# Beacon attention and soft mixture of experts on one Trainium2 core: V stored as two keys a partition, masks added by TensorE, experts in column groups

## The chip, the cores and the metric

One core of a Trainium2 chip runs the whole program. The metric is device time in microseconds. The engines are TensorE (PE, with its weight loads PEld), VectorE (DVE), ScalarE (ACT), GpSimd (POOL) and SyncE (SP, which issues most DMAs).

## The reference

Attention over 8 batches and 8 heads of 576 tokens with 64 dimensions; 16 beacon keys and values stand ahead of the others and are never masked. Its output, as 4608 rows of 512, is x for a soft mixture of 8 experts with 4 slots each:

```python
k_all = np.concatenate([beacon_k, k], axis=2)          # 592 keys
v_all = np.concatenate([beacon_v, v], axis=2)
scores = scale * np.matmul(q, k_all.transpose(0, 1, 3, 2))
scores = np.where(causal, -1000000000.0, scores)       # causal[:, Nb:] = triu(k=1)
a = softmax(scores, -1)
attn_out = np.matmul(a, v_all)
x = attn_out.transpose(0, 2, 1, 3).reshape(B * S, H * D)
logits = x @ phi                                       # 4608 x 32
d = softmax(logits, 0)                                 # over the tokens
slot_input = (d.T @ x).reshape(E, S_per_e, D)
slot_out[e] = np.maximum(slot_input[e] @ w1[e], 0.0) @ w2[e]    # 512 -> 1024 -> 512
c = softmax(logits, 1)                                 # over the slots
return c @ slot_out
```

## The kernel before

The kernel is one loop over 32 pairs of heads (`n`, four pairs `g` to a batch `b`) and a tail. The instructions of each engine run in the order in which the Python text issues them, so this order is written by hand; engines wait for each other only through the tiles they share.

**Loads.** `load_pair` (L84, DMAs at L88) brings q and k of one pair as 128 partitions of nine rows each, 288 KB a tensor; five pairs are held, and pair n+5 is asked for at the end of pair n. `load_v` (L96, L103) brings V as 128 keys a partition block, 8 heads of 64 values each, so that a DMA moves rows of 256 bytes; a quarter of the next batch is asked for at each pair of the present one. `cast_v` (L241) turns V to 16 bits into `vh`, partly on GpSimd and partly on VectorE, one pair after it was asked for. `load_w` (L109, L120) brings the experts' weights in 32 pieces of 512 KB (as stored in 16 bits), issued by GpSimd; six tiles for w1 and six for w2 hold 24 pieces, and the last eight take the place of pieces that experts 0 and 1 have used.

**A pair.** `transp(n+1)` (L187) transposes the next pair's q and k with 36 products of 64x64 into two PSUM tiles, which VectorE copies (L189) into `qT` and `kT`; GpSimd puts the beacon keys in front (L192). `score` (L202) has four steps, and every step fills one of two PSUM tiles `sc` and is followed by one exp on ScalarE (L208) of 1024, 992, 928 and 416 columns (two heads together). Keys lie on the partitions and queries on the columns. Step 0 holds the four full diagonal blocks, and GpSimd clears their masked half after the exp (L210); step 1 begins with the last diagonal block of 80, cleared at L216. `attend` (L229) multiplies the blocks of `ex` with V for one head of the pair before, 15 products into a PSUM tile `av`; column 64 of V holds ones, so that column 64 of the result is the softmax's sum, and VectorE divides (L236, L237) into `xb`. The order on TensorE in a pair is: score step 0, some routing, score step 1, the next pair's transposes, `attend` of the first head of the pair before, score step 2, `attend` of the second head, score step 3.

**Routing of a batch** runs in the next batch's pairs as seven pieces: three transposing `xb` into `xT` (L256, L261, L265), two for the logits and their exp `eLh` (L271, L275), one transposing that (L283), and `si_piece` (L294, L298), which adds `d.T @ x` to `siacc`.

**Tail.** The column sums for `c` (L373); then for each expert 32 products of w1's blocks with four slots each (L392), Relu into a zero-padded tile `hTz` (L395), and eight products of `hTz` with 512 columns of w2 (L397), all accumulated in one PSUM tile `sop`, which is `avs[0]`. VectorE scales it into `soh` (L401). The output is 36 products of 512 columns (L413), read out by ScalarE and VectorE in turn (L415, L417) and stored by SP in nine groups of four.

Of the kernel before, what the change touches and what calls it, by code (L numbers as in the profile page):

```python
# [17 lines left out]
def kernel(  # L18
# [24 lines left out]
    NP = B * H // 2  # L43
    NDC = Dm // P
    NFC = F // P
    DD = D + 1
    scale = 1.0 / D ** 0.5
    assert Dm == H * D and N == B * S and UL == 80 and J == 9
# [3 lines left out]
    steps = [  # L52
        [(c, P, P * c, P, P * c) for c in range(4)],
        [(4, UL, 4 * P, UL, 0), (3, P, 4 * P, UL, UL), (1, P, 2 * P, U - 2 * P, 2 * UL)],
        [(0, P, P, U - P, 0)],
        [(2, P, 3 * P, U - 3 * P, 0)],
    ]
    width = [512, 496, 464, 208]
    soff = [0, 512, 1008, 1472]
    EW = 1680  # L60
    blk = {}
    for st, pieces in enumerate(steps):
        for (c, kn, u0, un, col) in pieces:
            for i in range(NCH):
                lo = P * i
                if u0 <= lo < u0 + un:
                    blk[(c, i)] = soff[st] + col + lo - u0
    assert len(blk) == 15

    const = ctx.enter_context(tc.tile_pool(name="const", bufs=1))  # L70
    qkp = ctx.enter_context(tc.tile_pool(name="qkp", bufs=5))
    vfp = ctx.enter_context(tc.tile_pool(name="vfp", bufs=6))
    exq = ctx.enter_context(tc.tile_pool(name="exq", bufs=2))
    sml = ctx.enter_context(tc.tile_pool(name="sml", bufs=4))
    wh = ctx.enter_context(tc.tile_pool(name="wh", bufs=6))
# [5 lines left out]

    qf, kf = {}, {}

    def load_pair(n):  # L84
        b, g = divmod(n, H // 2)
        for (d, src, nm) in ((qf, q, "qf"), (kf, k, "kf")):
            t = qkp.tile([P, J, D], FP, name=nm, tag=nm)
            nc.sync.dma_start(  # L88
                out=t[:, :, :],
                in_=src[b, 2 * g:2 * g + 2].rearrange("h s d -> (h s) d").rearrange(  # L90
                    "(p j) d -> p j d", j=J))
            d[n] = t

    vf = {}

    def load_v(b, part):  # L96
        for c in ((0, 1), (2,), (3,), (4,))[part]:
            vf[(b, c)] = vfp.tile([P, H, D], FP, name="vf", tag="vf")
            if c == 0:
                nc.sync.dma_start(out=vf[(b, c)][0:Nb], in_=beacon_v[b].rearrange("h n d -> n h d"))  # L100
            lo, hi = max(0, c * P - Nb), min(S, (c + 1) * P - Nb)
            p0 = lo + Nb - c * P
            nc.sync.dma_start(out=vf[(b, c)][p0:p0 + hi - lo],  # L103
                              in_=v[b, :, lo:hi, :].rearrange("h p d -> p h d"))

    NPC = 4 * E
    w1h, w2h = {}, {}

    def load_w(m):  # L109
        e, r = divmod(m, 4)  # L110
        d, nm = (w1h, "w1h") if r < 2 else (w2h, "w2h")
        if r % 2 == 0:
            d[e] = wh.tile([P, 4096], F16, name=nm, tag=nm)
        o = (r % 2) * 2048
        if r < 2:
            src = moe_w1[e, r * 256:(r + 1) * 256].rearrange("(c p) f -> p c f", p=P)
        else:
            src = moe_w2[e, (r - 2) * 512:(r - 1) * 512].rearrange("(c p) f -> p c f", p=P)
        c = src.shape[1]
        nc.gpsimd.dma_start(  # L120
            out=d[e][:, o:o + 2048].rearrange("p (c f) -> p c f", c=c), in_=src)

    load_pair(0)
    bkf = const.tile([P, B, D], FP, name="bkf")
    nc.sync.dma_start(out=bkf[:, :, :], in_=beacon_k.rearrange("b h n d -> (h n) b d"))
    load_pair(1)
    for part in range(4):
        load_v(0, part)
    phif = const.tile([P, NDC, NSL], FP, name="phif")
    nc.sync.dma_start(out=phif[:, :, :], in_=moe_phi.rearrange("(c p) e -> p c e", p=P))  # L130
    load_pair(2)
    load_pair(3)
    load_pair(4)
# [5 lines left out]
    nc.vector.tensor_copy(out=idh[:, :], in_=idb[:, :])  # L139
    ones = const.tile([P, 1], F16, name="ones")  # L140
    nc.vector.memset(ones[:, :], 1.0)
    qT = [const.tile([P, 5 * P], BF, name=f"qT{i}") for i in range(3)]
    kT = [const.tile([P, 5 * P], BF, name=f"kT{i}") for i in range(3)]
    for i in range(3):
        nc.vector.memset(qT[i][:, 0:Nb], 0.0)
    vh = [const.tile([P, NCH, H, DD], F16, name=f"vh{i}") for i in range(2)]
    for i in range(2):
        nc.gpsimd.memset(vh[i][:, :, :, D:DD], 1.0)
    xb = [const.tile([P, NCH, H, D], F16, name=f"xb{i}") for i in range(2)]
    eLh = const.tile([NSL, Nb + N], F16, name="eLh")  # L150
    nc.vector.memset(eLh[:, 0:Nb], 0.0)
    dsum9 = const.tile([NSL, 2 * B], FP, name="dsum9")
# [4 lines left out]
    phih = const.tile([P, NDC, NSL], F16, name="phih")  # L157
    bkT = const.tile([P, NP, Nb], BF, name="bkT")
# [4 lines left out]
    nc.vector.memset(scs[1][64:P, :, 0:UL], 0.0)  # L163

    def beacons():
# [7 lines left out]
        for r in range(2):  # L173
            nc.vector.tensor_copy(
                out=bkT[64 * r:64 * r + 64, :, :],
                in_=tp[64 * r:64 * r + 64, :, :].rearrange(
                    "p b (g r n) -> p (b g) r n", g=H // 2, r=2)[:, :, r, :])


    def transp(n):  # L180
        for (f, dst) in ((qf, qT[n % 3]), (kf, kT[n % 3])):
            t = f.pop(n)
            tp = ps_tr.tile([P, J, 64], BF, name="tr", tag="tr")
            for j in range(J):
                for po in (0, 64):
                    hi = t[po:po + 64, j, :].bitcast(BF)[:, 1::2]
                    nc.tensor.transpose(tp[po:po + 64, j, :], hi,  # L187
                                        idb[po:po + 64, po:po + 64])
            nc.vector.tensor_copy(  # L189
                out=dst[:, Nb:Nb + S].rearrange("p (s j) -> p s j", j=J),  # L190
                in_=tp[:, :, :].rearrange("p j s -> p s j"))
        nc.gpsimd.tensor_copy(out=kT[n % 3][:, 0:Nb], in_=bkT[:, n, :])  # L192
# [3 lines left out]
    def score(n, st):  # L196
        if st == 0:
            ex[n] = exq.tile([P, 2, EW], F16, name="ex", tag="ex")
        sc = scs[st % 2]
        for (c, kn, u0, un, col) in steps[st]:  # L200
            for a in range(2):
                nc.tensor.matmul(  # L202
                    sc[0:kn, a, col:col + un],
                    kT[n % 3][64 * a:64 * a + 64, P * c:P * c + kn],
                    qT[n % 3][64 * a:64 * a + 64, u0:u0 + un],
                    start=True, stop=True)
        w, o = width[st], soff[st]
        nc.scalar.activation(ex[n][:, :, o:o + w], sc[:, :, 0:w], AF.Exp, scale=scale)  # L208
        if st == 0:
            nc.gpsimd.affine_select(  # L210
                out=ex[n][:, :, 0:512].rearrange("p a (c t) -> p a c t", c=4),
                in_=ex[n][:, :, 0:512].rearrange("p a (c t) -> p a c t", c=4),
                compare_op=AL.is_ge, fill=0.0, base=0,
                pattern=[[0, 2], [0, 4], [1, P]], channel_multiplier=-1)
        if st == 1:
            nc.gpsimd.affine_select(  # L216
                out=ex[n][0:UL, :, o:o + UL], in_=ex[n][0:UL, :, o:o + UL],
# [3 lines left out]
    def attend(n, a):  # L221
        b, g = divmod(n, H // 2)
        h = 2 * g + a
        for i in range(NCH):
            m = P if i < 4 else UL
            for c in range(i + 1):
                kn = P if c < 4 else UL
                o = blk[(c, i)]
                nc.tensor.matmul(  # L229
                    avs[a][0:m, i * DD:(i + 1) * DD],  # L230
                    ex[n][0:kn, a, o:o + m],
                    vh[b % 2][0:kn, c, h, :],
                    start=(c == 0), stop=(c == i))
# [77 lines left out]
    wl = 0  # L311
# [141 lines left out]
```

## Time and profile before

| | |
|---|---|
| runs | 236.87, 238.39 and 239.73 us, median 238.39 |
| profiled execution, span | 239.4 us |
| busy time in it | PE 187.1, PEld 129.1, DVE 130.8, ACT 127.4, POOL 89.4 us |
| DMA | 55.63 MB written, 63,715 packets, 41,920 of them under 512 B |
| first exp, last exp of the loop | start 11.56 us, end 173.4 us |
| experts | from 181.45 to 211.2 us |
| output | from 211.2 us to the end |

The page gives the profiled execution by its span, from the first instruction to the last. Its parts are one execution's; the runs are others. Busy times of engines lie beside each other and don't add up to the span, and a product's length holds a latency that the next one overlaps, so what a run of products costs is read from start to start.

### The profile page before, as it was taken

To read this page: it belongs to the slowest core of one execution; us is meant where nothing else is said; L and a number is where in the kernel's file an instruction comes from. 1 tells how busy PE (TensorE), PEld (TensorE's weight loads), DVE (VectorE), ACT (ScalarE), POOL (GpSimd) and SP (SyncE) were. 2 spreads that over 40 slices of the span, in tenths; PEclk is the share of its full clock that TensorE was granted. 3 is DMA by queue.
4 is the path that set the end of the run, shared out by engine and by line. 5 is a ranking of instruction groups with operands and counts; after the bars stand their busy time and mean duration, and the time that the engine had idled before them with its cause. 6 is when DMAs were issued, how large, how long until landed. Compare 5 with 4: busy or idle time off the path is not lost.

```text
span 239.4 us, 8048 instructions
## 1 busy us (share of the span) xinstructions
PE 187.1 (78%) x3512; PEld 129.1 (54%) x3512; DVE 130.8 (55%) x304; ACT 127.4 (53%) x187; POOL 89.4 (37%) x161
## 2 busy tenths in 40 slices
PE   0579778869986898797898698899869999979800
PEld 0457566647664766575666476677646445532200
DVE  4583967555777566777667666566652000058800
ACT  2075576747767487776786758477710000057700
POOL 4080645442652732744645363443542420000000
PEclk9999889985999799999999979689996569995555
DMA  6999999999899899999999999272599999919995
GB/s 193 225 300 281 317 225 243 298 258 240 220 248 228 193 230 282 205 273 263 258 317 262 230 201 277 43 127 41 92 161 202 209 206 210 159 81 422 416 413 248
DMA packets 63715, 55.63 MB, mean 232 GB/s; under 512 B 41920, under 2 KB 50112, under 8 KB 62656
## 3 DMA queue, kind: packets, MB, share of 16 engines
q1 hardware_dynamic: 50880, 38.35, 56.3%
q0 software_dynamic: 12800, 16.78, 41.5%
q8 instruction: 27, 0.44, 0.8%
q14 instruction: 8, 0.07, 0.1%
HBM read 62.46 MB, written 9.44 MB: 300 GB/s over the span
## 4 chain that ended last, share of the span: by engine, by line
PE 47%; DMA 16%; ACT 13%; DVE 5%; SPq 5%; POOL 5%; issue 4%; ACTq 0%
DMA vf<-in_v_dram 14%; ACT ex L208 10%; PE av_152 L397 8%; PE sc_156 L202 6%; PE av_152 L229 6%; PE tr L187 6%; PE fp L413 5%; PE tr L256 3%; DVE xT L261 3%; PE tr L392 3%; PE sc_157 L202 3%; SPq L103 3%; PE tr L271 2%; PE av_153 L229 2%; DMA kf<-in_k_dram 2%
## 5 line engine op out<-in xcount | busy, mean ns | idle before, releaser
L208 ACT ACTIVATE ex<-sc_156 128x1024 f16<-128x1024 f32 x64 | 63.0, 984 | 47.4 <-PE sc_156 L202 47.2
L208 ACT ACTIVATE ex<-sc_157 128x992 f16<-128x992 f32 x64 | 48.0, 751 | 12.2 <-PE sc_157 L202 12.1
L210 POOL TENSOR_SCALAR_AFFINE_SELECT ex<-ex 128x1024 f16<-128x1024 f16 x32 | 34.9, 1092 | 46.9 <-ACT ex L208 46.9
L229 PEld LDWEIGHTS <-ex 128*128 128x128 f16 (+2 forms) x960 | 40.6, 113 | 12.8 <-issue 10.9
L397 PE MATMUL av_152<-w2h,hTz 128*32 128x512 f16 x64 | 20.1, 471 | 2.3 <-ACT hTz L395 2.3
L187 PE MATMUL tr<-idb,kf 64*64 64x64 bf16 x576 | 16.6, 204 | 2.0 <-issue 0.8
L261 DVE COPY xT<-tr 128x1024 f16<-128x1024 f16 x16 | 10.5, 687 | 13.2 <-PE tr L256 13.2
L187 PEld LDWEIGHTS <-qf 64*64 64x64 bf16 x576 | 13.4, 118 | 7.4 <-issue 6.2
L187 PE MATMUL tr<-idb,qf 64*64 64x64 bf16 x576 | 16.8, 205 | 0.6 <-DMA qf<-in_q_dram 0.5
L395 ACT ACTIVATE hTz<-tr 128x32 f16<-128x32 f32 x8 | 1.6, 198 | 28.8 <-PE tr L392 28.8
L401 DVE TENSOR_SCALAR soh<-av_152,rd 32x512 f16<-32x512 f32 x1 | 0.7, 737 | 29.0 <-PE av_152 L397 29.0
L187 PEld LDWEIGHTS <-kf 64*64 64x64 bf16 x576 | 14.3, 119 | 2.9 <-issue 2.6
L413 PE MATMUL fp<-soh,eLh 32*128 32x512 f16 x36 | 14.1, 522 | 1.4 <-DVE soh L401 0.8
L415 ACT ACTIVATE osb<-fp,rc 128x512 f32<-128x512 f32 x18 | 11.8, 687 | 5.9 <-PE fp L413 5.6
L202 PE MATMUL sc_156<-qT_129,kT_132 64*128 64x128 bf16 (+1 forms) x110 | 9.6, 276 | 6.9 <-POOL kT_132 L192 4.8
L243 POOL CAST vh_138<-vf 128x512 f16<-128x512 f32 (+1 forms) x12 | 7.7, 639 | 19.0 <-DMA vf<-in_v_dram 19.0
L216 POOL TENSOR_SCALAR_AFFINE_SELECT ex<-ex 80x160 f16<-80x160 f16 x32 | 10.6, 331 | 10.7 <-ACT ex L208 10.3
L202 PEld LDWEIGHTS <-kT_132 64*128 64x128 bf16 (+1 forms) x198 | 8.6, 110 | 11.1 <-POOL kT_132 L192 5.7
L417 DVE TENSOR_SCALAR osb<-fp,rc 128x512 f32<-128x512 f32 x18 | 13.1, 748 | 2.4 <-PE fp L413 1.6
L120 POOL DMA_DIRECT2D w1h<-in_moe_w_dram x16 | 11.5, 724 | 6.6 <-PE tr L392 6.6
L120 POOL DMA_DIRECT2D w2h<-in_moe_w_dram x16 | 12.1, 758 | 4.4 <-PE av_152 L397 4.4
L229 PE MATMUL av_153<-vh_138,ex 128*128 128x65 f16 (+2 forms) x240 | 11.5, 202 | 2.1 <-issue 2.1
(206 smaller groups left out, 318.9 us busy)
## 6 DMA issues: line engine op xcount, KB each, us to landing
qf<-in_q_dram SPq DMA_DIRECT2D x32, 288.0 KB, 6.2
kf<-in_k_dram SPq DMA_DIRECT2D x32, 288.0 KB, 6.3
w1h<-in_moe_w_dram POOLq DMA_DIRECT2D x16, 512.0 KB, 8.6
w2h<-in_moe_w_dram POOLq DMA_DIRECT2D x16, 512.0 KB, 8.9
out_dram<-osb SPq DMA_DIRECT2D x8, 1024.0 KB, 8.2
vf<-in_v_dram SPq DMA_DIRECT2D x24, 256.0 KB, 7.0
vf<-in_v_dram SPq DMA_DIRECT2D x8, 224.0 KB, 6.9
vf<-in_v_dram SPq DMA_DIRECT2D x8, 160.0 KB, 7.2
```

The costliest lines, as they stand in the source:

```text
L120: nc.gpsimd.dma_start(out=d[e][:, o:o + 2048].rearrange("p (c f) -> p c f", c=c), in_=src)
L187: nc.tensor.transpose(tp[po:po + 64, j, :], hi, idb[po:po + 64, po:po + 64])
L202: nc.tensor.matmul(sc[0:kn, a, col:col + un], kT[n % 3][64 * a:64 * a + 64, P * c:P * c + kn], qT[n % 3][64 * a:64 * a + 64, u0:u0 + un], ...
L208: nc.scalar.activation(ex[n][:, :, o:o + w], sc[:, :, 0:w], AF.Exp, scale=scale)
L210: nc.gpsimd.affine_select(out=ex[n][:, :, 0:512].rearrange("p a (c t) -> p a c t", c=4), in_=ex[n][:, :, 0:512].rearrange("p a (c t) -> p ...
L216: nc.gpsimd.affine_select(out=ex[n][0:UL, :, o:o + UL], in_=ex[n][0:UL, :, o:o + UL], compare_op=AL.is_ge, fill=0.0, base=0, pattern=[[0, ...
L229: nc.tensor.matmul(avs[a][0:m, i * DD:(i + 1) * DD], ex[n][0:kn, a, o:o + m], vh[b % 2][0:kn, c, h, :], start=(c == 0), stop=(c == i))
L261: nc.vector.tensor_copy(out=xT[b][:, :, P * cs[0]:P * cs[0] + 2 * P].rearrange("p t (i u) -> p i t u", i=2), in_=tp[:, :, :, :])
L397: nc.tensor.matmul(sop[0:NSL, :], hTz[:, e, t, :], w2h[e][:, t * Dm:(t + 1) * Dm], start=(e == 0 and t == 0), stop=(e == E - 1 and t == NF ...
L413: nc.tensor.matmul(fp_[:, :], etok(cg, j), soh[:, :], start=True, stop=True)
L415: nc.scalar.activation(osb[:, j, :], fp_[:, :], AF.Copy, scale=rc[:, i:i + 1])
L417: nc.vector.tensor_scalar(out=osb[:, j, :], in0=fp_[:, :], scalar1=rc[:, i:i + 1], scalar2=None, op0=AL.mult)
```

## The change

q and k come in quads of heads (`load_quad`, 128 partitions of two heads' nine rows, three quads held). A transpose takes 128 partitions by 64 columns, and heads 0 and 1 of the quad go to partitions 0 to 63 of the result, 2 and 3 to the other half; `transp` is split into groups of four and five row blocks, and one tensor is done in each pair. A pair `n` now means heads a and a+2 of a quad.

V lies as two consecutive keys a partition, so that a DMA's rows are 512 bytes, for keys 0 to 511; the last 80 keys lie as before. The scores of a group of 256 keys are therefore made for even and for odd keys, with a stride of two over `kT`'s columns. A diagonal block needs both halves of a group, so the fifteen blocks are cut anew: steps 0 and 1 hold keys 0 to 255 against queries from 128 on, steps 2 and 3 hold the first 128 queries of each group with its first 128 keys in natural order, and keys 256 to 511 against queries from 384 on; step 3 has the last block. `lift_v` copies V of those first 128 keys to natural order (`vup`). Instead of the large select on GpSimd, TensorE adds a mask of -8e9 to the scores by products with a constant (`eup`, `mg`, or `idb`, `mf`); the select of the last block stays.

The experts take the slots as stationary and the weights as moving operand: `layer1` makes four products of 512 columns, one for each quarter of the 512 inputs, into four groups of 32 partitions, twice; ScalarE and VectorE copy the result, and `layer2` sums the four groups and transposes by a product with `sel`, applies Relu, and multiplies by w2 into four groups of 32 partitions of `sop`. The four groups are summed in the output's product, for which `phi` is repeated four times and `eLh` and `soh` have 128 partitions. Weights are held in 22 tiles of a piece, and six more pieces take q's and k's tiles as these come free; the last four wait for expert 0. Routing is in one slot a pair, and the output is stored in 18 groups of two.

```diff
     def load_v(b, part):
...
+            nc.sync.dma_start(out=t[lo:P],
+                              in_=v[b, :, k0:k1, :].rearrange("h (p s) d -> p h (s d)", s=2))
...
+        if NW <= m < NW + 6:
+            t = qkp.tile([P, J * P * 2], F16, name="wx", tag=("qf", "kf")[m % 2])
+        else:
+            t = wh.tile([P, 2048], F16, name="w", tag="w")
...
+    def transp(m, which, grp):
...
+        for j in range(j0, j1):
+            for h in range(2):
+                hi = t[:, h, j * D:(j + 1) * D].bitcast(BF)[:, 1::2]
+                nc.tensor.transpose(tp[64 * h:64 * h + 64, j - j0, :], hi, idb[:, :])
...
     def score(n, st):
...
+        if r == 1:
+            for h in range(2):
+                nc.tensor.matmul(sc[:, h, 0:P], idb[:, :], mf[:, :], start=True, stop=False)
+            for h in range(2):
+                hh = slice(64 * h, 64 * h + 64)
+                for z in range(2):
+                    nc.tensor.matmul(
+                        sc[64 * z:64 * z + 64, h, 0:P],
+                        kt[hh, a, 256 * s + z:256 * s + z + 127:2],
+                        qt[hh, a, 256 * s:256 * s + P], start=False, stop=True)
+        w = U - 256 * r - P
+        for h in range(2):
+            hh = slice(64 * h, 64 * h + 64)
+            nc.tensor.matmul(
+                sc[:, h, g0:g0 + w], kt[hh, a, 256 * r + s:256 * r + s + 255:2],
+                qt[hh, a, 256 * r + P:U], start=True, stop=False)
+        for h in range(2):
+            hh = slice(64 * h, 64 * h + 64)
+            nc.tensor.matmul(sc[:, h, g0:g0 + P], eup[hh, :], mg[hh, s, :],
+                             start=False, stop=True)
...
-        if st == 0:
+        if st == 3:
             nc.gpsimd.affine_select(
...
+    def lift_v(b, r):
+        vb = b % 2
+        for s in range(2):
+            nc.vector.tensor_copy(out=vup[vb][64 * s:64 * s + 64, r, :, 0:D],
+                                  in_=vm[vb][0:64, r, s, :, 0:D])
...
+    def routing(n):
+        b, g = divmod(n, 4)
+        if g == 3:
+            w = [lambda: xt_piece(b, 0), lambda: xt_piece(b, 1)]
+            return ([lambda: dt_piece(b - 1)] if b > 0 else []) + w
+        if b == 0:
+            return []
+        if g == 1:
+            return [lambda: xt_piece(b - 1, 2), lambda: xt_piece(b - 1, 3)]
+        if g == 2:
+            return [lambda: logit_piece(b - 1, 0), lambda: logit_piece(b - 1, 1)]
+        return [lambda: si_piece(b - 2)] if b > 1 else []
...
+        want = min(NW, int(0.72 * n)) if n < 26 else min(NW + 6, 18 + int(1.7 * (n - 25)))
...
+        score(n, 0)
+        score(n, 1)
+        if nq < NQ:
+            transp(nq, n % 2, 0)
...
+            cast_v(0, 0, nc.gpsimd)
+            cast_v(0, 1, nc.vector)
+            cast_v(0, 2, nc.gpsimd)
+            lift_v(0, 0)
+            lift_v(0, 1)
+            for r in range(4):
+                nc.vector.tensor_copy(out=phih[:, :, r, :], in_=phif[:, :, :])
         if n >= 1:
             attend(n - 1, 0)
+        score(n, 2)
+        if nq < NQ:
+            transp(nq, n % 2, 1)
+        work = routing(n)
+        for w_ in work:
+            w_()
+        score(n, 3)
         if n >= 1:
             attend(n - 1, 1)
+        if n % 2 == 0 and n // 2 + 3 < NQ:
+            load_quad(n // 2 + 3)
+        if b + 1 < B:
+            if g == 0:
+                load_v(b + 1, 0)
+            if g == 1:
+                load_v(b + 1, 1)
+                load_v(b + 1, 2)
+            if g == 2:
+                cast_v(b + 1, 0, nc.gpsimd)
+            if g == 3:
+                cast_v(b + 1, 1, nc.gpsimd)
+                cast_v(b + 1, 2, nc.gpsimd)
+                lift_v(b + 1, 0)
+                lift_v(b + 1, 1)
+        for _ in range(nload[n]):
+            load_w(wl)
+            wl += 1
...
+    def layer1(e):
+        h1 = scs[e % 2]
+        for hf in range(2):
+            for c in range(NDC):
+                nc.tensor.matmul(h1[32 * c:32 * c + 32, hf, :], siT[:, c, :],
+                                 w1c(e, c, hf * 512, 512), start=True, stop=True)
+        t = exq.tile([P, 2, EW], F16, name="h1s", tag="ex")
+        nc.scalar.activation(t[:, 0, 0:512], h1[:, 0, :], AF.Copy)
+        nc.vector.tensor_copy(out=t[:, 1, 0:512], in_=h1[:, 1, :])
...
+    def layer2(e):
+        hp = ps_tr.tile([P, NFC, SPE], FP, name="tr", tag="tr")
+        for f in range(NFC):
+            nc.tensor.matmul(hp[:, f, :], t[:, f // 4, (f % 4) * P:(f % 4 + 1) * P],
+                             sel[:, e * SPE:(e + 1) * SPE], start=True, stop=True)
+        nc.scalar.activation(hTz[:, e, :, e * SPE:(e + 1) * SPE], hp[:, :, :], AF.Relu)
+        for f in range(NFC):
+            c = f % 4
+            nc.tensor.matmul(sop[32 * c:32 * c + 32, :], hTz[:, e, f, :], w2c(e, f),
+                             start=(e == 0 and f < 4), stop=(e == E - 1 and f >= 4))
...
+    layer1(0)
+    free_w(NW + 8)
...
+    for e in range(1, E):
+        layer1(e)
+        layer2(e - 1)
+        free_w(NPC)
+    layer2(E - 1)
```

## The prediction

> **What bounds the kernel now.** I read the page first, then busy time by stage, the chain and the waits, then the timeline of a few stretches. From the page:
>
> ```profile
> span 239.4 us, 8048 instructions
> ...
> PEclk9999889985999799999999979689996569995555
> DMA  6999999999899899999999999272599999919995
> ...
> q1 hardware_dynamic: 50880, 38.35, 56.3%
> q0 software_dynamic: 12800, 16.78, 41.5%
> ...
> DMA vf<-in_v_dram 14%; ACT ex L208 10%; PE av_152 L397 8%; PE sc_156 L202 6%; PE av_152 L229 6%; PE tr L187 6%; PE fp L413 5%; PE tr L256 3%; DVE xT L261 3%; PE tr L392 3%; PE sc_157 L202 3%; SPq L103 3%; PE tr L271 2%; PE av_153 L229 2%; DMA kf<-in_k_dram 2%
> ```
>
> The slices are 6 us each. DMA is full from slice 1 to 24, so the attention loop runs beside saturated transfers, and the largest entry of the chain is V's arrival. By stage (columns: stretch, length, busy time of each engine, granted clock, DMA share, GB/s):
>
> ```profile
> 118.00:138.00 20.00, 15.82 (x379) 11.94 (x381) 13.42 (x33) 13.60 (x20) 9.44 (x18) 0.99 1.13 264
> 158.00:171.00 13.00, 11.72 (x259) 8.71 (x257) 9.03 (x24) 9.76 (x15) 4.94 (x10) 1.00 0.38 59
> 180.50:196.00 15.50, 14.64 (x162) 7.06 (x161) 1.12 (x7) 0.59 (x3) 5.78 (x8) 0.56 1.18 207
> 196.00:211.20 15.20, 13.73 (x196) 7.63 (x193) 0.00 (x0) 0.99 (x5) 0.00 (x0) 1.00 0.95 165
> ```
>
> At 158 us the loads of q, k and v are over and TensorE is still busy 90%: without DMA pressure the loop is TensorE's. From 180.5 the experts are TensorE's alone, half of that at about half clock. The waits give the loop's stalls:
>
> ```profile
> ACT ex L208 <- PE sc_156 L202: 47.2, 53, 9.5
> DVE soh L401 <- PE av_152 L397: 29.0, 1, 29.0
> POOL vh_138 L243 <- DMA vf<-in_v_dram: 19.0, 7, 5.8
> POOL vh_137 L243 <- DMA vf<-in_v_dram: 9.5, 5, 4.3
> ```
>
> ScalarE waits for scores, and GpSimd, which casts V and also masks `ex`, waits 28.5 us for V. The first exp of pair 4 starts at 31.74, that of pair 20 at 114.14, of pair 21 at 117.58, and the last exp ends at 173.4. So 28 pairs take 141.7 us, 5.06 each. Undisturbed stretches have 3.44 us for a pair without routing (114.14 to 117.58) and about 4.75 with (160.05 to 164.79), 4.42 over a batch of four. The stalls are the other 0.64 us a pair.
>
> **What TensorE's parts cost.** A stretch at full clock (start, length, line; from one start to the next is what a run holds the engine):
>
> ```profile
> 166.27 0.47 PE L187 MATMUL tr<-idb,qf 64*64 64x64 bf16 x18
> 166.62 0.47 PE L187 MATMUL tr<-idb,kf 64*64 64x64 bf16 x18
> 167.03 0.67 PE L229 MATMUL av_152<-vh_138,ex 128*128 128x65 f16 x15
> 167.63 0.37 PE L202 MATMUL sc_156<-qT_128,kT_131 64*128 64x464 bf16 x2
> 167.93 0.67 PE L229 MATMUL av_153<-vh_138,ex 128*128 128x65 f16 x15
> 168.54 0.26 PE L202 MATMUL sc_157<-qT_128,kT_131 64*128 64x208 bf16 x2
> ```
>
> Scores of 464 and of 208 columns last 0.37 and 0.26 us, so a column costs 0.11/256, 0.42 ns. Two scores of 464 columns hold the engine 0.30 us (167.63 to 167.93): one stream of 0.195 and 0.105 for the change of shape; the two row halves run together. 18 transposes of 64 columns take 0.35 us, 39 ns a pair, against 27 ns for one stream alone, so two of those overlap too. 15 products of `attend` take 0.60.
>
> **The change, part by part.**
>
> *Loop, TensorE per pair.* `attend` keeps 15 products a head: 1.21. The scores stream 464+128 columns in steps 0 and 1 (mask included): 0.25 each. Steps 2 and 3 each have the full mask, two products of 128 that use all rows and cannot pair (0.11), four 64x64 products (0.11), a pair of 208 (0.09), a mask pair (0.055) and two changes of shape (0.21): 0.57, and step 3 has one more pair of 80 (0.08). Sum 1.72 with a change behind; before it was 1.2. Transposes: 18 of 128 columns instead of 36 of 64. They write to different column halves; if these overlap, 9 x 0.055 = 0.50 and two changes 0.2, 0.70 as now (0.35+0.41); if not, 0.5 more. I take the overlap, from the 39 ns a pair above. Routing, four pairs' share: 20 transposes x 40 ns, eight logits x 123 ns, 20 products x 28 ns and changes, 3.0/4 = 0.75. Together 1.21+1.72+0.70+0.75 = 4.4 us, and 4.5 with one change back to step 0. ScalarE's exps have the same 3360 columns, 3.44 a pair, and 0.3 for logits: under 4.5 and hidden.
>
> [...]
>
> *Loop, other engines.* GpSimd loses the 1.09 us select of every pair and keeps the 0.33 one; it gains casts of 128x1024, at 0.615 for 512 about 1.2 each, two a batch, and more DMA issues (0.74 each, 0.72 of them a pair). DVE swaps two casts a batch for four copies (`lift_v`), 0.2 to 0.5 each, which wait for GpSimd's cast: one is queued behind the cast that is only issued at the end of the fourth pair, behind the last select, and transposes' evictions stand behind it on DVE. I put 1 us a batch, 0.25 a pair, on that. Bounds: 0, and the 3.1 us that such a wait cost at 33.36 us in the trace, 0.8 a pair. V is now asked for two pairs before its cast instead of one; at 7 us to landing (5.3 to 10.3) against 4.8 us a pair it was late, and against 9.5 it is seldom late. The loop: 4.5+0.25 = **4.75 us a pair**, ends 4.4 and 5.3.
>
> *Does DMA still fit?* Output ran at 416 GB/s, 22.7 us for 9.44 MB. q1's 56.3% is 134.8 us; less the output, 112. q and k at the output's rate are 45 us, V 67 for 9.7 MB: 256-byte rows cost 1.5 times as much. Rows of 512 B halve the packets of 86% of V: between nothing and 29 us saved, I take 20, nearer the packet count since short packets show the surcharge. Weights: 99.4 us for 32 pieces, 3.1 each, or 2.5 by the 207 GB/s above. Counted so the old loop has 45+67+20 x 3.1 = 174 us in some 156 us of real time, the overlap being counted twice; with that factor 0.9 the new one, 45+47+28 x 3.1, needs 161, until about 163 us. The loop ends then too, and late weights belong to late experts. So DMA is no longer ahead of TensorE, but there is no slack either.
>
> [...]
>
> *Start.* k needs 1.44 MB landed before the first score instead of 0.58, and pair 0 waits for the second quad behind V; against that, three quads reach further than five pairs. The trace gives 230 GB/s in the first 17 us: pair 0 starts 1 us later, and `phih`'s copies on DVE wait behind quad 1 and V, but pair 4 starts at 31.5, within 2 of now. On SP no later load waits longer: a quad's buffer is free one pair before it is asked for.
>
> *Drain,* last exp to first expert: 8.05 us now. The 36 column sums (1.3) move behind `layer1(0)`; one `si_piece` (0.65) enters, half of it under the last normalisation: 7.4.
>
> *Experts,* 29.75 now (181.45 to 211.2):
>
> ```profile
> 196.97 1.90 PE L397 MATMUL av_152<-w2h,hTz 128*32 128x512 f16 x8 [0.29 <-ACT hTz L395]
> 198.80 0.95 PE L392 MATMUL tr<-siT,w1h 128*128 128x4 f16 x32
> 199.79 0.20 ACT L395 ACTIVATE hTz<-tr 128x32 f16<-128x32 f32 x1 [2.88 <-PE tr L392]
> ```
>
> Eight products of 512 columns hold 1.83 us, one 0.215; at half clock 3.6. An expert becomes 8 of these in `layer1`, 8 small ones, Relu, and 8 in `layer2`, each eight in two sets of four column groups. If a set costs one stream: 0.43+0.1 twice, small ones 0.3, Relu gap 0.34 (198.80+0.9 to the next product): 1.7 us, or 2.7 at half clock. If groups run one after another: 4.3. The trace has no four groups at once; nearest are the pairs that overlap, so I take one stream. All at full clock 8 x 1.7+1.3 = 14.9; with the 13.7 us of half clock that the present stage begins with, 19.5. I take 18. The last pieces (28 to 31) go out 1 and 5 us into the stage, 1.5 us to issue two, 5 to 9 to landing: there by 15, before expert 7 needs them at 16.
>
> *Output:* 28.2 us, DMA-bound, the same bytes; unchanged.
>
> **Sum:** 31.5 + 28 x 4.75 (133.0) + 7.4 + 18 + 28.2 = 218.1, against 239.4 for the profiled execution. Its span lies inside the three runs and 1.0 above their median; so I forecast **217 us**.
>
> **Rivals.**
> - *Column groups do not overlap (slower).* One mechanism in two places: transposes +0.5 x 28 = 14, experts +2.6 x 8 = 21 and about 3 more at half clock: 255 us. For: no four groups in the trace. Against: the transposes' 39 ns a pair. It turns the sign when some 60% of that loss comes true. Chance 0.08.
> - *The loop gains nothing.* DMA stays the bound at 5.06 a pair (V's packets cost by bytes, weights displace V): +8.7, 226. For: no slack in the DMA sum. Against: longer lead of V, shorter GpSimd queue. Chance 0.2.
> - *Last pieces late.* The resident 28 help, but the slowest landing (15.7 us) holds expert 7 to 22 us into the stage: 222. Chance 0.05.
> - *Better than forecast.* The loop at 4.45 with no stall from `lift_v`, and experts at full clock early: -8.4 - 3.1, 206. For: denser TensorE work. Against: the half clock of 180.5 to 196 with TensorE 94% busy. Chance 0.2.
>
> [...]
>
> **Numbers.** Forecast 0.47, rivals as above. A measurement of this kernel (236.9 to 239.7) tells about 1% from no change. Every case but the first rival is faster by over 1%; its 0.08, and 0.05 for partial forms of it, go to slower and same. Range 204 to 234: from below the best case to well past 226.
>
> **What would show it.** Right: exp of [464] twice at 0.93, first exps 4.7 us apart; packets under 512 B down from 41,920 to about 9,000; no V wait on GpSimd over 3 us; `sop` and `h1` sets of four products 0.22 apart at full clock; experts some 18 us. Wrong: four products each 0.215 apart in a set; transposes 55 ns apart singly; DMA landings of V above 12 us; first exps more than 5 us apart.

## The result, and the profile after

The changed kernel takes **250.35 us** (median of four runs, 248.65 to 251.12) against 239.06 (236.87 to 239.77) for the kernel before: 1.050 times as long, with a 95% interval of 1.042 to 1.057. The forecast was 217 us, so it has the wrong sign.

One correction first: in the text on the change, `vup` is said to hold V in natural order. It holds the even keys of a block in partitions 0 to 63 and the odd keys in 64 to 127; the full diagonal blocks of the scores lie the same way. No number hangs on it.

The page of the profiled execution after the change:

```profile
span 249.1 us, 7374 instructions
...
PEclk9999999999999799979999997999799955557955
DMA  6999999999998998999799979645999999109997
...
DMA packets 47640, 55.59 MB, mean 223 GB/s; under 512 B 8440, under 2 KB 33016, under 8 KB 47608
...
q1 hardware_dynamic: 34808, 38.34, 54.1%
...
PE av L303 14%; PE sc L265 11%; PE tr L231 8%; DVE vup L323 7%; DVE kT L232 5%; DMA qf<-in_q_dram 5%; DVE qT L232 4%; PE sc L258 4%; DMA w<-in_moe_w_dram 3%; PE tr L335 3%; PE sc L254 3%; PE sc L270 3%; PE fp L543 2%; DVE xb L308 2%; PE tr L345 2%
```

The packets are as planned: 8,440 are under 512 B, where there were 41,920, and V's arrival, 14% of the chain before, is not in the last line any more. But the transfers of queue q1 take as long as before, 54.1% of 249.1 us against 56.3% of 239.4, 134.8 us both times. In the chain stand VectorE's copies now: `vup` (the new `lift_v`) 7%, `kT` 5%, `qT` 4%. And the clock row has single slices of 7 in the loop and four of 5 where the experts are.

Busy time by stretch (length, busy time of PE, PEld, DVE, ACT and POOL, granted clock, DMA share, GB/s). First a loop stretch that was also shown of before, then the middle of the experts:

```profile
118.00:138.00 20.00, 17.50 (x347) 12.66 (x344) 14.22 (x34) 12.98 (x17) 6.39 (x12) 1.00 1.00 230
...
205.00:220.00 15.00, 12.31 (x144) 4.05 (x132) 3.46 (x6) 3.63 (x11) 0.00 (x0) 0.50 0.57 95
```

The whole loop from pair 4 on, of the kernel before and then of the changed one:

```profile
31.74:173.41 141.67, 120.06 (x2687) 91.08 (x2686) 93.53 (x228) 98.35 (x141) 68.49 (x123) 0.93 0.99 218
```

```profile
37.00:191.50 154.50, 136.25 (x2498) 96.87 (x2494) 106.36 (x247) 101.23 (x140) 46.84 (x86) 0.96 1.00 211
```

TensorE is busy 16.2 us more than before, and its idle time, most of which was to go, falls only from 21.6 us to 18.25. Its waits in the changed kernel (in total, times, longest; in us) say where:

```profile
PE tr L335 <- DVE kT L232: 8.9, 14, 0.8
PE tr L368 <- DVE qT L232: 7.7, 6, 1.3
...
PE tr L345 <- DVE qT L232: 2.0, 6, 0.3
```

These three are 18.6 us over the span, all but 0.6 of them in the loop: nearly the whole of its idle time. L335, L368 and L345 are the routing pieces (`xt_piece`, `si_piece`, `logit_piece`), and what they wait for is VectorE's copy out of the transposes' tile. By segments of the span, against the sum of the prediction and the kernel before:

| us | before | sum | after |
|---|---|---|---|
| start to pair 4's first exp | 31.7 | 31.5 | 37.0 |
| 28 pairs, to the last exp | 141.7 | 133.0 | 154.6 |
| last exp to first expert | 8.0 | 7.4 | 6.7 |
| experts | 29.7 | 18 | 22.3 |
| output | 28.2 | 28.2 | 28.5 |

The experts give 7.4 us and the drain 1.3; the loop takes 12.9 and the start 5.2.

### The profile page after: what moved, and what is told of

It is laid out like the page before. It is cut to its first block, busy times and chain, and to the rows that moved or that the text cites. A ratio compares the mean times of both kernels' runs of the same rounds, so it can differ in the third digit from the quotient of the medians.

```text
span 249.1 us, 7374 instructions
## 1 busy us (share of the span) xinstructions
PE 196.7 (79%) x3192; PEld 127.3 (51%) x3192; DVE 152.2 (61%) x348; ACT 134.4 (54%) x195; POOL 60.1 (24%) x117
## 2 busy tenths in 40 slices
DMA packets 47640, 55.59 MB, mean 223 GB/s; under 512 B 8440, under 2 KB 33016, under 8 KB 47608
## 3 DMA queue, kind: packets, MB, share of 16 engines
q1 hardware_dynamic: 34808, 38.34, 54.1%
## 4 chain that ended last, share of the span: by engine, by line
PE 57%; DVE 22%; DMA 8%; issue 3%; ACT 3%; SPq 1%; DVEq 0%; ACTq 0%
PE av L303 14%; PE sc L265 11%; PE tr L231 8%; DVE vup L323 7%; DVE kT L232 5%; DMA qf<-in_q_dram 5%; DVE qT L232 4%; PE sc L258 4%; DMA w<-in_moe_w_dram 3%; PE tr L335 3%; PE sc L254 3%; PE sc L270 3%; PE fp L543 2%; DVE xb L308 2%; PE tr L345 2%
## 5 line engine op out<-in xcount | busy, mean ns | idle before, releaser
L278 ACT ACTIVATE ex<-sc 128x928 f16<-128x928 f32 (+2 forms) x128 | 107.9, 870 | 70.3 <-PE sc L275 41.1
L265 PE MATMUL sc<-qT,kT 64*128 64x464 bf16 (+1 forms) x256 | 43.6, 340 | 1.5 <-DVE kT L232 1.0
L303 PE MATMUL av<-vm,ex 128*128 128x65 f16 (+1 forms) x768 | 40.7, 203 | 0.0
L308 DVE TENSOR_TENSOR xb<-av,r 128x320 f16<-128x320 f32 x64 | 31.5, 492 | 2.2
L232 DVE COPY kT<-tr 128x512 bf16<-128x512 bf16 (+1 forms) x32 | 24.9, 779 | 12.7 <-PE tr L231 12.7
L307 DVE RECIPROCAL r<-av 128x5 f32<-128x5 f32 x64 | 12.0, 188 | 31.9 <-PE av L303 31.7
L232 DVE COPY qT<-tr 128x512 bf16<-128x512 bf16 (+1 forms) x32 | 24.8, 776 | 9.7 <-PE tr L231 9.3
L270 PE MATMUL sc<-mg,eup 64*128 64x128 bf16 x256 | 30.4, 231 | 0.0
L129 POOL DMA_DIRECT2D w<-in_moe_w_dram x26 | 19.3, 742 | 7.3 <-PE sc L476 5.5
L303 PE MATMUL av<-vup,ex 128*128 128x65 f16 x128 | 20.0, 204 | 0.3 <-ACT ex L278 0.3
L335 PE MATMUL tr<-idh,xb 128*128 128x128 f16 (+1 forms) x160 | 12.7, 215 | 9.3 <-DVE kT L232 8.9
L323 DVE COPY vup<-vm 64x512 f16<-64x512 f16 x32 | 18.5, 579 | 0.4
L254 PE MATMUL sc<-mf,idb 128*128 128x128 bf16 x128 | 18.6, 228 | 0.1
L335 PEld LDWEIGHTS <-xb 128*128 128x128 f16 (+1 forms) x160 | 9.7, 97 | 11.1 <-issue 9.6
```

The lines of the kernel that those rows point to most:

```text
L129: nc.gpsimd.dma_start(out=t[:, 0:2048].rearrange("p (c f) -> p c f", c=c), in_=src)
L232: nc.vector.tensor_copy(out=dst[:, :, Nb:U].rearrange("p a (s j) -> p a s j", j=J)[:, :, :, j0:j1], in_=tp[:, :, :].rearrange("p j (a s) - ...
L254: nc.tensor.matmul(sc[:, h, 0:P], idb[:, :], mf[:, :], start=True, stop=False)
L265: nc.tensor.matmul(sc[:, h, g0:g0 + w], kt[hh, a, 256 * r + s:256 * r + s + 255:2], qt[hh, a, 256 * r + P:U], start=True, stop=False)
L270: nc.tensor.matmul(sc[:, h, g0:g0 + P], eup[hh, :], mg[hh, s, :], start=False, stop=True)
L303: nc.tensor.matmul(av[0:m, i * DD:(i + 1) * DD], l, r_, start=(x == 0), stop=(x == len(ops) - 1))
```

## The theory, and its rivals

A stretch of TensorE in a first pair of a batch (start, length, line) and in the pair behind it:

```profile
127.28 0.47 PE L231 MATMUL tr<-idb,qf 128*64 128x128 bf16 x10
129.00 0.65 PE L368 MATMUL tr<-dT,xb 128*128 128x32 f16 x20 [1.25 <-DVE qT L232]
...
133.46 0.43 PE L335 MATMUL tr<-idh,xb 128*128 128x128 f16 x5
134.45 0.42 PE L335 MATMUL tr<-idh,xb 128*128 128x128 f16 x5 [0.56 <-DVE kT L232]
```

VectorE at that time:

```profile
125.74 2.46 DVE L323 COPY vup<-vm 64x512 f16<-64x512 f16 x4
128.23 0.72 DVE L232 COPY qT<-tr 128x512 bf16<-128x512 bf16 x1
128.85 0.17 DVE L307 RECIPROCAL r<-av 128x5 f32<-128x5 f32 x1
...
133.57 0.83 DVE L232 COPY kT<-tr 128x640 bf16<-128x640 bf16 x1 [0.22 <-PE tr L231]
```

**Theory: two waits on one pair of tiles.** Transposes and routing share two rotating PSUM tiles `tr`. In the new order the routing pieces stand right behind the second group of transposes. The second `xt_piece` of a pair asks for the tile whose copy (0.83 us, 133.57) has just begun: 0.5 to 0.7 us in nearly every such pair. In the first pair of a batch VectorE has also the four copies of `lift_v` ahead (2.46 us from 125.74), both groups' copies are late, and TensorE waits 1.25 to 1.33 us. Everything behind stands too, because TensorE's instructions run in the order of the text. In four of the six batches with such a long wait, a window of 3.41 us at half clock follows it (from 83.8, 107.7, 152.0 and 175.9 us).

**Rivals.** DMA is still the bound of the loop (its share is 1.00 there) and the waits only fill its time. Or TensorE's own products are dearer than forecast (masks, changes of shape). For the experts: the half clock, or the new order of products itself.

## Experiments

All edits are to the changed kernel, but for the experts alone, which go into the kernel before. A time without a range is that of a single run. Kernels 6 and 9 are those of experiments 6 and 9.

**1. Routing ahead of the second group of transposes.**

```diff
             attend(n - 1, 0)
+        work = routing(n)
+        for w_ in work:
+            w_()
         score(n, 2)
         if nq < NQ:
             transp(nq, n % 2, 1)
-        work = routing(n)
-        for w_ in work:
-            w_()
         score(n, 3)
```

> The changed kernel with one edit: the routing pieces stand ahead of score step 2 instead of behind the second group of transposes. Theory A (the routing waits for one of the two tr tiles, which the eviction of the transposes just ahead of it still holds, 0.5 to 1.3 us in each pair that has routing): this wait goes, a pair with routing falls from about 5.4 to 4.7 us, the loop by some 16 us and the span from 249 to about 233. Rival B (the loop goes at the pace of the saturated DMA): the loop moves by less than 4 us, since the bytes are the same. Rival C (the added mask products and shape changes fill TensorE): less than 4 us too, and TensorE shows no idle time ahead of the routing either way.

Measured: 238.28 us (237.44 to 241.99), 1.001 times the kernel before (0.996 to 1.006); the loop from pair 4 on falls from 154.6 to 143.2. TensorE's idle time in it falls from 18.25 to 10.6 us, and its busy time from 136.25 to 132.4, because no half-clock window is left in the loop (clock 1.00 from 35 to 178 us). The wait for `lift_v` is still there, now at the transposes, and no half clock follows it here:

```profile
PE tr L231 <- DVE qT L232: 7.4, 7, 1.2
```

So the place of the routing costs 11.4 us, about what the change had lost against the kernel before: 7.6 us of idle time, and 3.9 us of busy time that goes with the half clock. (A new wait of 2.8 us, of `xt_piece` for `dT`, is in what is left.)

**2. No `lift_v` from the third batch on** (`vup` keeps an older batch's V).

```diff
-                lift_v(b + 1, 0)
-                lift_v(b + 1, 1)
+                if b == 0:
+                    lift_v(b + 1, 0)
+                    lift_v(b + 1, 1)
```

> The changed kernel with the four copies of lift_v left out from the third batch on, so that V of an earlier batch is used there. Theory A, with the copies (0.58 us each, and waiting for GpSimd's cast) as the reason why the first pair of a batch waits 1.3 us instead of 0.5 to 0.7: 0.7 us less in six batches, and perhaps the half-clock windows that follow these waits in four batches, 1.2 us each; span 240 to 245. Rival B (DMA's pace): no change over 2 us.

Measured: 236.67 us, loop 142.6. The wait of `si_piece` (7.7) is gone, that of `xt_piece` (8.9) unchanged. So the copies cost 12.0 us. TensorE's idle time in the loop falls to 11.2 us and its busy time to 131.4, for the half-clock windows are gone here too (clock 1.00 from 34.2 to 176.8 us). So these windows stand in both prices, which are therefore not two separate shares of the loop, though their sum is 23.4 us, as much as both waits together cost (experiment 9 against 3).

**3. 28 of the 32 weight loads left out.**

```diff
     def load_w(m):
         e, r = divmod(m, 4)
+        if m >= 4:
+            wt[m] = wt[r]
+            return
```

> The changed kernel with only expert 0's four weight pieces loaded and used for all experts; 28 of 32 weight loads are left out. Rival B (the loop goes at DMA's pace): without 24 MB or more of reads beside it the loop falls by 15 us or more. Theory A (PSUM tile waits in the loop, half clock in the experts): the loop falls by less than 3 us and the expert stage stays within 1 us of 22.3, for the last pieces were not late; span 246 to 249.

Measured: 247.73 us; the loop lasts 154.4 us instead of 154.6, with the same waits (8.9, 7.5 and 2.0). With 14.7 MB fewer to bring the loop is the same: DMA is not what bounds this kernel's loop, although its share is 1.00.

**4. Fillers in the experts.** Nine products of 128x128x512 in the drain (left out below) and two per expert while it waits for Relu, into a tile that nobody reads.

```diff
+    def fill(x, k_):
+        for _ in range(k_):
+            nc.tensor.matmul(avs[1][:, :], idh[:, :], wt[x][:, 0:512], start=True, stop=True)
...
         nc.scalar.activation(hTz[:, e, :, e * SPE:(e + 1) * SPE], hp[:, :, :], AF.Relu)
+        fill(4 * e + 2, 2)
```

> The changed kernel with products of 128x128 by 512 added whose result nobody reads: nine in the drain after the loop, and two for each expert in the gap in which TensorE waits for Relu. Theory D (the expert stage of 22.3 us is at half clock throughout because TensorE has gaps of about 0.5 us in each 2.7, and full clock would make it 15): with the gaps filled the clock rises and the stage falls to 15 to 18 us, span 242 to 246. Rival (the clock does not answer to that, or the stage is bound by its chain of evictions and Relu): the stage grows by the fillers at half clock, 2 x 0.43 less the 0.5 gap, to 25 us, span 250 to 254.

Measured: 244.60 us; expert stage 17.3 instead of 22.3. One expert of the changed kernel, and then one with the fillers (L482):

```profile
204.42 1.05 PE L492 MATMUL av<-w,hTz 128*32 128x512 f16 x8 [0.49 <-ACT hTz L489]
205.24 1.07 PE L476 MATMUL sc<-w,siT 128*32 128x512 f16 x8
206.25 0.37 PE L487 MATMUL tr<-sel,h1s 128*128 128x4 f16 x8
207.10 1.05 PE L492 MATMUL av<-w,hTz 128*32 128x512 f16 x8 [0.48 <-ACT hTz L489]
```

```profile
202.00 0.61 PE L505 MATMUL av<-w,hTz 128*32 128x512 f16 x8
202.45 0.60 PE L488 MATMUL sc<-w,siT 128*32 128x512 f16 x8
202.98 0.35 PE L499 MATMUL tr<-sel,h1s 128*128 128x4 f16 x8
203.20 0.59 PE L482 MATMUL av<-w,idh 128*128 128x512 f16 x2
203.84 0.62 PE L505 MATMUL av<-w,hTz 128*32 128x512 f16 x8
```

From one `av` to the next it is 2.68 us without fillers, with a gap of half a microsecond at Relu, and 1.84 with them, although more work is done: eight products of 512 columns in two sets of four hold TensorE 0.82 us (204.42 to 205.24) and then 0.45 (202.00 to 202.45). That is the clock, 0.53 over the stage before and 1.00 now. So the four column groups run together, and the stage is long because of its clock. The last pieces of the weights were a little late: TensorE waits 0.5 us for them in the changed kernel and 1.2 us here.

**5. The new experts alone, in the kernel before** (`layer1`, `layer2`, `phi` repeated four times; loop, masks, V and the 24 resident pieces as before).

> The kernel before with the experts' part of the change alone: layer1 and layer2 in column groups, phi repeated four times, eLh and soh over 128 partitions. The loop, V, the masks and the 24 resident pieces stay as before. Theory: the four column groups overlap, an expert takes 2.7 us at half clock and the stage, 29.75 us before, falls to 22 to 25, the upper end where the last eight pieces arrive late; span 231 to 234. Rival (what the experts gain they owe to the 28 resident pieces): the last eight pieces set the stage's end at 28 us or more, span 237 or more.

Measured: 239.41 us, 1.006 times the kernel before (0.997 to 1.014); stage 28.7 instead of 29.7. The stage (first line) and what its TensorE waits for:

```profile
179.70:208.40 28.70, 19.01 (x196) 6.19 (x194) 6.10 (x10) 5.70 (x16) 5.78 (x8) 0.50 1.10 192
```

```profile
PE sc L396 <- DMA w1h<-in_moe_w_dram: 4.8, 2, 2.9
```

The chain of this stage is 60% the loads of w2: the last eight pieces, asked for only when experts 0 and 1 are done, take the place of the products. At half clock and with late pieces the cheaper expert is worth 1.0 us here, 7.4 together with the 28 resident pieces.

**6. Both waits removed, fillers added.** Routing ahead of `score(n, 2)`, its pieces divided around `attend`; two of the four `lift_v` copies on GpSimd behind the casts, the other two singly behind routing on VectorE; the fillers of 4. The main lines:

```diff
+        work = routing(n)
+        if len(work) == 3:
+            work.pop(0)()
         if n >= 1:
             attend(n - 1, 0)
+        for w_ in work:
+            w_()
+        if g == 3 and b + 1 < B:
+            lift_v(b + 1, 0, 1, nc.vector)
+        if g == 0 and b >= 1:
+            lift_v(b, 1, 1, nc.vector)
         score(n, 2)
...
                 cast_v(b + 1, 0, nc.gpsimd)
+                lift_v(b + 1, 0, 0, nc.gpsimd)
...
                 cast_v(b + 1, 2, nc.gpsimd)
-                lift_v(b + 1, 0)
-                lift_v(b + 1, 1)
+                lift_v(b + 1, 1, 0, nc.gpsimd)
```

> The changed kernel with the three edits together, nothing left out: routing ahead of score step 2 and its first piece of three ahead of attend; lift_v split, half of it on GpSimd right behind its casts, the other half on VectorE in a later pair than the cast; fillers in the drain and the experts. Theory A: each pair comes to 4.7 to 4.8 us, the loop from pair 4 to 133 (154.6 in the changed kernel), experts 17 to 18: span 221 to 225. Rival B (a bound under the waits shows up, DMA or VectorE): the loop stays at 140 or more, span 228 or more.

Measured: **222.72 us** (221.09 to 223.82), 0.937 times the kernel before (0.926 to 0.948). It beats both kernels. Loop 134.4, experts 16.2. What ends work late now (in the loads' line, KB each and median us to landing; 8.4 in the kernel after):

```profile
vs<-in_v_dram SPq DMA_DIRECT2D x8, 512.0 KB, 14.5
```

```profile
POOL vm L315 <- DMA vs<-in_v_dram: 7.7, 5, 3.1
```

Six of the loop's seven batches last 17.0 to 19.6 us, the sixth of the program 22.05.

**7. The same, and a start in another order**: q ahead of the beacon keys, the second quad ahead of V, the copies of `phi` three pairs later.

```diff
+    load_quad(0, (0,))
     nc.sync.dma_start(out=bkf[:, :, :], in_=beacon_k.rearrange("b h n d -> (h n) b d"))
-    load_quad(0)
+    load_quad(0, (1,))
+    load_quad(1)
     load_v(0, 0)
     load_v(0, 1)
-    load_quad(1)
```

> As e6a_waits_removed, with the start reordered: q of quad 0 first, then the beacons and k, quad 1 ahead of V, and the copies of phi in pair 3 instead of pair 0. Theory: the second quad's q arrives before pair 0 needs it, and VectorE does not stand for phi; pair 4 begins at 33 to 34.5 us instead of about 35.5: 1 to 3 us less than e6a_waits_removed. Rival: V comes later by as much and the first attend waits for it: no difference.

Measured: 223.18 us (220.82 to 229.52), 0.936 (0.924 to 0.947): no difference. In its trace the first exp comes at 13.18 instead of 13.52; but the traced execution is the longest of the four runs, so no later time of it is set against kernel 6.

**8. Kernel 6 without mask products** (the masked scores count in full).

> As e6a_waits_removed, with TensorE's mask products (eup with mg, idb with mf) left out, so that only the last block is masked. Theory C (in a loop bound by TensorE the masks cost what they hold the engine, some 0.17 each time eup and mg follow and 0.2 for idb with mf, 1.0 us a pair at most): the loop falls until ScalarE's 3.75 us a pair or VectorE stops it, by 0.4 to 0.8 us a pair, 11 to 22 us in all. Rival: less than 4 us, and the masks were hidden beside ScalarE.

Measured: 219.87 us; the loop is as long as in kernel 6 (134.3). The second batch of the program, which has no wait for V, lasts 17.0 us instead of 18.55, so the masks cost TensorE about 0.4 us a pair; but GpSimd now waits 19.8 us for V (longest 6.5) and V's arrival is 36% of the chain. What the masks cost could not be had in this kernel: V is late then.

**9. Kernel 6 without 28 weight loads.**

> The kernel with the routing moved forward, the lifts split and the fillers added, with 28 of its 32 weight loads left out (all experts multiply with the first expert's weights; the output is another one). What is left of its loop: 134.35 us from pair 4's first exp, one batch of 22.05 among batches of 19.05, and 7.7 us of waits for V on GpSimd. Theory (with TensorE's waits gone, DMA is the next bound, because weights and V share it): V's waits fall below 1 us, the long batch goes back to about 19, loop 130 to 132, V's landings back below 10 us. Rival (the long batch has another cause, and TensorE's own work is the loop): loop 134 with the long batch still there, as the 28 loads changed nothing in the kernel after.

Measured: 217.01 us. The loop:

```profile
33.50:164.50 131.00, 130.79 (x2498) 94.08 (x2497) 92.95 (x233) 100.97 (x140) 37.34 (x77) 1.00 0.71 171
```

TensorE is busy 130.79 of 131.00 us, and the five batches with full routing last 19.04 to 19.06 each. That is TensorE's own work: 4.76 us a pair there, 4.68 over all 28. Its 2,498 products are the ones that took 136.25 us of busy time after the change. So the loop of the changed kernel is accounted for: 130.8 of work, 5.5 for half-clock windows, 18.2 of waits. The same loads that cost nothing in experiment 3 cost 3.4 us here. The batch of 22.05 is gone.

**10. Kernel 6 with its loads spaced wider** (0.6 pieces a pair up to pair 24, 2.4 from there).

```diff
-        want = min(NW, int(0.72 * n)) if n < 26 else min(NW + 6, 18 + int(1.7 * (n - 25)))
+        want = min(NW, int(0.6 * n)) if n < 25 else min(NW + 6, 14 + int(2.4 * (n - 24)))
```

> The same kernel with all loads, but the weight loads spaced wider in the loop (0.6 a pair instead of 0.72 up to pair 24, 2.4 a pair behind it). Theory (V is late in the sixth batch because weights displace it): V's waits fall by half, the batch of 22.05 us becomes 19 to 20, loop 132, span 218; the weights come no later than the experts need them. Rival (the bytes have to go somewhere: as many us of late weights in the expert stage, or q, k late at the end): loop 132 but expert stage 2 us longer, span 220 as before.

Measured: 225.45 us (224.56 to 226.34), 0.940 times the kernel before (0.929 to 0.951); loop 134.5, experts 20.6. The rival is right about the experts: V's waits on GpSimd fall from 7.7 to 2.3 us, but TensorE waits 4.0 us for weights in the expert stage. The loop gains nothing, against both: the sixth batch of the program falls from 22.05 to 19.05, but the third takes 22.2. It has a pause of 1.57 us in the middle of `attend` to which the view gives no releaser ("issue"), and a half-clock window behind it (clock 0.79 from 62 to 70 us):

```profile
62.82 0.36 PE L303 MATMUL av<-vm,ex 128*128 128x65 f16 x5 [1.57 <-issue]
```

Kernel 6 has such a pause in its long batch too (1.50 us, to 124.21), next to one of 1.26 that does come from V; so V's lateness is only about half of that batch's 3.0 us. The kernel before has one of 2.14 us, to 52.46. Its DMA records have a transfer of 16 KB on the queue q8, of kind "instruction" on the page, that ended at 50.96, 1.5 us before TensorE went on; the trace has 27 such transfers. What held TensorE is not shown. That the loads bring such pauses on fits experiment 9, without 28 loads and without a pause, but no run shows it singly.

## Why the prediction was wrong

**The loop: 154.6 instead of 133.0.** The step that failed is the one that let TensorE's products run one behind the other. *Routing* was put in at its length, 0.75 us a pair, and nothing was said of the place to which it moved: behind the second group of transposes, with two `tr` tiles for both. The instruction to ask about was the eviction of 0.83 us on VectorE, and the profile of before has its kind (L189, 0.75 us). Price 11.4 us, 0.41 a pair, with no term or bound in the prediction. *`lift_v`* was named, with its queue: 0.25 a pair, bounds 0 and 0.8. It cost 12.0 us, 0.43 a pair. The queue of evictions behind the copies was right. The wait for GpSimd's cast was not: the copies start beside the casts.

```profile
125.78 1.04 POOL L315 CAST vm<-vs 128x1024 f16<-128x1024 f32 x1
126.76 0.68 POOL L318 CAST vlh<-vl 80x512 f16<-80x512 f32 x1
```

The first copy took 1.22 us (from 125.74), the second 0.61 (from 126.97), the two behind the casts 0.29 each, against 0.2 to 0.5 forecast. In both prices the half-clock windows, 4 to 5 us of each, had no term in the prediction.

**4.75 us a pair could be had**: 4.68 in experiment 9, 4.76 in its full batches. But that is TensorE's work alone, which the prediction had at 4.5, so this term was some 0.2 too small, and that it meets the forecast's 4.75, which has 0.25 for `lift_v` in it, is luck. By kernel 6's timeline scores cost 2.1 instead of 1.72, transposes 0.75 (0.70), `attend` 1.1 (1.21), routing as forecast. Steps 0 and 1 take 0.78 together instead of 0.50: from the start of a mask pair to the next product 0.16 to 0.22 us pass (86.91 to 87.07, 81.55 to 81.77 in kernel 6), where a stream of 128 columns was counted as 0.055. Behind step 0 that product has the mask's form (64*128), so that the lost time is a change of shape, for which the prediction put 0.105 us by its own estimate, is not shown.

**DMA** was counted as having no slack and ending with the loop. The 20 us that rows of 512 B were to save did not come: q1 takes 134.8 us as before, and by the DMA records a packet of V lasts 22 ns with 256 B and 44 ns with 512. (The remark that 256-byte rows cost 1.5 times as much does not follow from its own figures either: 67 us against 23 at the output's rate is 2.9 times. By the DMA records of the kernel before a byte of V in packets of 256 B took 1.8 times as long as a byte of q and k: 22 ns a packet against 109 for 2,304 B.) For the changed kernel the missing 20 us did not show (experiment 3), because the waits had made the loop longer. Where they are gone, the statement becomes true: 131.0 with fewer loads, 134.4 with all, and no gain without masks. V's landing was 8.4 to 9.7 us, within the lead of 9.5 that was counted on, but for 0.2; the one wait of GpSimd for it, 3.2 us, is at the start, and none is left in the loop.

**The experts: 22.3 instead of 18.** The prices per expert were good (forecast 2.7 at half clock and 1.7 at full, measured 2.68 and 1.84, in which the fillers are). The step that failed is "13.7 us of half clock, then full", carried over from the kernel before: there TensorE was busy 27.4 of 29.7 us, here 18.5 of 22.3, and the half clock lasts 27.3 us, from 199.8 to 227.1, past the end of the stage. The stretches at half clock in the loop are 3.41 us each, and this one is eight times that. That gaps of 0.5 us in 2.7 are what held the clock down fits experiment 4 (0.53 with them, 1.00 with fillers in them); but the kernel before had 13.7 us at half clock in a stage that was 92% busy (27.4 of 29.7), so the busy share alone doesn't decide. Whether the gaps or the shape of the products (32 columns of the array each, the fillers 128) do, the runs don't tell apart.

**The start: 37.0 instead of 31.5.** The first exp came 1.0 later than forecast (13.5). Pair 0 then waits 2.25 us for the second quad's q behind V, which the text named and did not price. Its products run at half speed at first: the same pair takes 0.57 us at 26.25, as long as in a recorded half clock of the kernel before (0.57 at 29.34, half clock from 28.2 to 31.6), and 0.37 from 31.25. The clock column reads 1.00 here, but the clock record of this trace only begins at 29.2. The kernel before has such a pair ahead of its record too (0.57 at 23.72, record from 24.8), so half speed at the start is not the change's own.

```profile
16.23 0.64 PE L231 MATMUL tr<-idb,qf 128*64 128x128 bf16 x8 [2.25 <-DMA qf<-in_q_dram]
...
26.25 0.57 PE L265 MATMUL sc<-qT,kT 64*128 64x464 bf16 x2
...
31.25 0.37 PE L265 MATMUL sc<-qT,kT 64*128 64x464 bf16 x2
```

How much of the 5.5 us is the change is not settled: experiment 2, whose code is the same up to pair 7, reached pair 4 at 34.2. There the wait for q is 1.3 us, and 2.8 us of this segment differ between executions of the same start.

**Right:** column groups overlap, the number of packets, V's landing, drain (6.7 for 7.4), output. Of the signs of being wrong one came: first exps more than 5 us apart (5.5). **Of the rivals** none was this: the only slower one was the overlap, which holds, and "the loop gains nothing" had DMA as its cause. A second slow rival, a wait of TensorE at the `tr` tiles, would have taken one question: who holds the tile that the moved piece writes?

## What to carry to other kernels

When a piece of work is moved in a hand-written order, look up which rotating buffer it writes, who empties the one ahead, and how long that takes, and put that time in as a term of its own; the length of the piece alone is not its price. Products added up back to back give what an order can reach at best (here 4.7 us a pair, and 5.5 with its waits); the waits are a sum of their own, and so is the half clock behind them. A cheaper stage has to be priced at the clock that it will get: the new experts ran at half clock but for the first 1.5 us, and products that do nothing made the stage 5 us shorter.

## What the runs showed of the hardware

- Half clock lasted through a stage with TensorE 83% busy (18.5 of 22.3 us, clock 0.53); with fillers it was 90% busy (15.6 of 17.3) at 1.00. A wait of 1.25 to 1.33 us in the loop of the kernel after was followed by 3.41 us at half clock in four batches of six. The clock records of that trace and of the one before begin whole multiples of 3.41 us apart; these four waits lie whole in the 3.41 us ahead of the half clock, the other two lie across such a border, with at most 0.98 us on one side. What decides is not shown: seven waits in experiment 1 (7.4 us together, the longest 1.2) and waits of 1.50 and 1.26 us in kernel 6 had no half clock behind them (1.00 over both loops), and the pause of 1.57 us in experiment 10 had.
- A DMA share of 1.00 did not mean that DMA was the bound: the loop lasted the same without 28 of 32 weight loads (154.4 us against 154.6). When less of TensorE stood in the way, V's landing rose from 8.4 to 14.5 us at the same bytes.
- A VectorE copy of 64x512 in 16 bits took 0.29 us behind GpSimd's casts (0.38 once in two of the batches), and 1.22 and 0.61 beside them (125.74 and 126.97 in the changed kernel; the other batches of its loop alike).
- Packets of 256 and of 512 B took the same time per byte (22 and 44 ns); half the packets did not make q1 faster (134.8 us both).
- TensorE stood for 1.50, 1.57 and 2.14 us (kernel 6, the one with loads spaced wider, the kernel before) with no releaser in the view. The last of these ended 1.5 us after a transfer of 16 KB on q8 (50.96 to 52.46); what held TensorE is not shown. Kernel 9, without 28 loads, had no such pause.
